# Router logits carried through the attention as eight extra columns, memory scaled on its way out of PSUM

## The chip, the cores and the metric

The kernel runs on one core of a Trainium2 chip. The metric is device time in microseconds, from one launch to its end, and lower is better. TensorE (PE in the profile) multiplies matrices, with its weight loads shown apart as PEld; VectorE (DVE), ScalarE (ACT) and GpSimd (POOL) work element by element; SyncE (SP) issues most transfers. Matrix products land in PSUM and are copied or consumed from there. PSUM buffers are few: the tag `pm` of the pool `ps_m` has one, so each user of it waits until the one before has been read.

## The reference, cut to what matters

Three layers follow each other over 4 x 576 = 2304 tokens of 512 values (8 heads of 64).

```python
scores = q @ k.T / 8, causal                      # per batch and head, 576 x 576
local  = softmax(scores) @ v                      # 576 x 64
mem    = (phi(q) @ M_prev) / (phi(q) @ z_prev + 1e-6)   # phi(x) = elu(x) + 1
x      = sigmoid(beta) * mem + (1 - sigmoid(beta)) * local
logits = (x / (|x| + 1e-6)) @ (emb / (|emb| + 1e-6)).T / tau    # 8 experts
token  -> argmax expert, gate = its softmax weight
out1   = gate * relu(x @ w1[e]) @ w2[e]
g      = h * clip(h + 3, 0, 6) / 6,  h = out1 @ w_in ;  out = g @ w_out
```

The routing needs, for each token, the product of its 512 values with eight expert directions. A row of x is a sum over heads of weighted value rows and memory rows, so these products can be formed before or after the attention's sums.

## The kernel before

**Attention, by pairs.** Sixteen pairs (four batches of four) of heads go through nine blocks each: 128 query rows at a time, five blocks for the first head (the fifth holds the last 64 rows of both heads) and four for the second. A block's scores (`mm` in `scores`, lines 291 to 310) go to PSUM, DVE takes the row maxima (`nmx`, line 314), ACT the exponentials (line 320), PE turns them by transposes (line 330), ACT copies the turned tile (`aT`, line 331), and PE sums values: `sumup`, line 344, with `aT` as weights and 65 columns of `vt` as the moving side (64 values and one column that gives the softmax's sum). The fifth block moves both heads' 130 columns. `finish` divides and adds the memory part into `xb` (lines 350 to 362).

**Memory.** `mem_pair` (line 260) forms phi(q) and multiplies it by `mz` (130 columns: 64 and the normaliser, for two heads), three row blocks in one `pm` tile and two in the next. ACT copies the first out of PSUM, DVE the second (line 274); DVE adds the small constant to the normaliser and inverts it (lines 278 and 279), and POOL multiplies the 128 x 640 tile (line 280).

**Routing.** After each pair `route_pair` (line 365) transposes the pair's 128 columns of `xb`, five blocks of rows (line 373), has them copied by ACT and DVE (line 377), and multiplies each by `enT`, the scaled directions, 8 columns wide (line 380, tile `plg`); DVE adds the result into `lgs`. After a batch's fourth pair `route` takes the norms (five ACT squares, a POOL power), scales the logits, finds the expert, and PE ranks the tokens (`prk`, lines 426 to 429) from the one-hot table `ohb` that DVE wrote at line 421. Then it scales `xb` by the gate and POOL scatters the rows. `totals` counts tokens with one more product, `pc`, line 471.

**What sets the order.** The Python loop at the end of `attention` counts steps, one for each block; in a step it issues scores five blocks ahead, a transpose, the sums of the block before, and one piece of each generator in `jobs` (memory) and of the first in `work` (routing); each `yield` ends a piece. A scheduler then reorders instructions on each engine by its own estimates, so code that is adjacent in the loop needn't be adjacent on an engine. Each engine runs its list in order: an instruction that waits holds all behind it. Transfers are issued by SP in order, eight in flight at most.

**Start.** SP loads pair 0, its values, `mz`, the embeddings and then pair 1. Pair 1 is split into high and low parts on ACT, DVE and POOL (`split_pair`, lines 235 to 258) before its scores.

**Feed-forward.** After the attention the first two slots of the experts run (`NEARLY`), and the last batch's routing and the tables of slots run beside them as `tail`, some pieces after each weight tile (`side`). PE is near full from there to the end.

An fp32 product appears as two PE instructions, so the 400 products of `sumup` are 800 rows in the profile, and `plg` has 160; a transpose is one.

Of the kernel before, what the change touches and what calls it, by code (L numbers as in the profile page):

```python
# [17 lines left out]
P = 128  # L18
# [22 lines left out]
EMB, ZERO, GATES, MEM0 = 1, 32, -3, -2  # L41
AT_LOAD, AT_VT, AT_SPLIT, AT_MEM = -19, -15, -11, -4
# [5 lines left out]
def build(nc, tc, qT, kT, v, Mz, beta, emb, tau, wm, w2, out, dbg=None):  # L48
# [31 lines left out]
def attention(nc, tc, rts, g):  # L80


    qT, kT, v, Mz, beta, emb, tau = (g[n] for n in ("qT", "kT", "v", "Mz", "beta", "emb", "tau"))
# [15 lines left out]
    vt_b = [ac.tile([P, NT, 2, D + 1], F32, name=f"vt{i}", tag=f"vt{i}") for i in range(H // 2)]  # L99
# [17 lines left out]

    def load_values(i):
# [6 lines left out]
    W = 2 * (D + 1)  # L125
# [4 lines left out]
    tau8 = ac.tile([E, 1], F32, name="tau8", tag="tau8")  # L130
    loads = {0: load_pair(0)}
# [48 lines left out]
    def gates():  # L180
# [7 lines left out]
        for i, vt in enumerate(vt_b):  # L188
            w = iomg[:, 2 * i:2 * i + 2]
            nc.vector.tensor_copy(vt[:, :4, :, D], w.unsqueeze(1).to_broadcast([P, 4, 2]))  # L190
            nc.vector.tensor_copy(vt[64:, 4, :, D], w[64:])
        for y in range(2):
            r = slice(64 * y, 64 * y + 64)
            z = mz[r, :, 65 * y + 64].rearrange("p (b h) -> p b h", b=B)
            nc.vector.tensor_tensor(z, z, igb[r, y::2].unsqueeze(1).to_broadcast([64, B, H // 2]), ALU.mult)

    enT = r1.tile([P, 4, E], F32, name="enT", tag="enT")

    def embeddings():
        esq = p2.tile([E, DM], F32, name="esq", tag="ph")  # L200
# [6 lines left out]
        nc.vector.tensor_scalar(emb_s, emb_s, ens, None, ALU.mult)  # L207
        pt = ps_m.tile([P, 512], F32, name="pte", tag="pm")
        for c in range(4):
            nc.tensor.transpose(pt[:, c * E:(c + 1) * E], emb_s[:, c * P:(c + 1) * P], ident[:E, :E])  # L210
        nc.vector.tensor_copy(enT.rearrange("p c e -> p (c e)"), pt[:, :4 * E])
# [48 lines left out]
    def mem_pair(i, qp, mem):  # L260
# [6 lines left out]
        nc.vector.tensor_copy(ph[:, S:], ph[:, 4 * P:S])  # L267
# [118 lines left out]
    def route(b, xb, lgs):  # L386
# [5 lines left out]
        for t in range(NT):  # L392
            nc.scalar.activation(sq, xb[:, t], AF.Square, accum_out=ss[:, t:t + 1])
            if t % 2:
                yield
# [748 lines left out]
```

## Time and profile before

| | us |
|---|---|
| median of 3 runs | 1027.35 (1025.5 to 1032.72) |
| the profiled execution | 1024.81 |
| its span, first to last instruction | 1023.1 |
| PE busy | 965.4 (94%) |
| DVE, ACT, POOL busy | 595.7, 503.2, 337.2 |
| mean granted TensorE clock | 0.974 of full speed |

A busy share of PE counts matmuls from start to modelled end, and they overlap, so the price of one is not its listed duration but the distance from one start to the next; the chain of waits shows that when it merges a run of them. The attention takes the first 297 us. The granted clock has two levels, 2.4 GHz (1.00) and 1.2 GHz (0.50).

### The profile page before, as it was taken

The numbers are of one execution on the slowest core, as the hardware profiler recorded it, in microseconds if no ns is written. First come the engines' busy times: TensorE is split into PE (matmuls) and PEld (weight loads), VectorE is DVE, ScalarE is ACT, GpSimd is POOL, SyncE is SP. The second block draws the span as 40 slices with busy tenths as digits, with TensorE's granted clock in tenths as the row PEclk, the third lists the DMA queues.
The fourth block names the chain that finished last, engine by engine and source line by source line (L and its number), as shares of the span: only waits on it lengthen the run. The fifth ranks groups of instructions, "written<-read, shape, count | busy, mean of one in ns | idle before, by whom it ended". The sixth has DMA issues, their size and how long they took to land.

```text
span 1023.1 us, 18922 instructions
## 1 busy us (share of the span) xinstructions
PE 965.4 (94%) x7054; PEld 890.4 (87%) x7054; DVE 595.7 (58%) x1456; ACT 503.2 (49%) x1036; POOL 337.2 (33%) x268
## 2 busy tenths in 40 slices
PE   8999799899988999899899999799999999999995
PEld 7789689788888999899899988789899999989994
DVE  6676867967857776776776896133333332333321
ACT  6678668767666653452454553233333333333331
POOL 4343634633425474672765235200000000000000
PEclk9799879979999999999999999999999999999998
DMA  9675555622168777877777800200000000000000
GB/s 212 149 168 107 141 123 125 163 65 66 68 231 273 262 238 249 301 248 262 285 258 264 281 28 1 3 22 21 3 19 22 1 21 1 22 1 21 22 1 23
DMA packets 75252, 122.03 MB, mean 119 GB/s; under 512 B 39048, under 2 KB 39048, under 8 KB 75152
## 3 DMA queue, kind: packets, MB, share of 16 engines
q1 hardware_dynamic: 71600, 111.29, 37.4%
q0 software_dynamic: 3552, 9.45, 2.6%
q8 instruction: 57, 0.93, 0.4%
q14 instruction: 43, 0.35, 0.1%
HBM read 107.55 MB, written 13.16 MB: 118 GB/s over the span
## 4 chain that ended last, share of the span: by engine, by line
PE 75%; DVE 9%; DMA 7%; issue 3%; ACT 3%; POOL 2%; SPq 1%; POOLq 0%; DVEq 0%; ACTq 0%
PE ph L796 8%; PE ph L795 8%; PE ph L794 8%; PE po L344 7%; PE po L1043 6%; PE po L1045 6%; PE po L1044 6%; PE ptr L330 4%; DMA perm<-tok,posi 3%; PE py L851 3%; PE py L849 3%; PE py L850 3%; PE ps L302 2%; PE plg L380 2%; PE pm L271 2%
## 5 line engine op out<-in xcount | busy, mean ns | idle before, releaser
L1063 DVE SCALAR_TENSOR_TENSOR t<-t,ph 128x256 f32<-128x256 f32 x144 | 60.4, 420 | 165.5 <-ACT t L1061 164.1
L1061 ACT ACTIVATE t<-ph,half 128x256 f32<-128x256 f32 x144 | 68.2, 473 | 162.1 <-PE ph L796 158.9
L786 POOL TENSOR_TENSOR lw<-rw,hw 128x1024 fp32r<-128x1024 f32 x50 | 119.9, 2403 | 77.5 <-ACT hw L785 67.8
L795 PE MATMUL ph<-xh,lo 128*128 128x256 f32 x480 | 134.3, 280 | 0.0
L796 PE MATMUL ph<-xl,hw 128*128 128x256 f32 x468 | 132.3, 283 | 0.0
L1032 POOL DMA_INDIRECT out<-ob,pmt x18 | 17.5, 972 | 346.5 <-DVE ob L1079 308.1
L794 PE MATMUL ph<-xh,hw 128*128 128x256 f32 x448 | 127.7, 285 | 1.8 <-ACT xh L804 1.8
L344 PE MATMUL po<-vt,aT 128*128 128x65 f32 (+1 forms) x800 | 115.6, 279 | 2.0 <-ACT aT L331 1.9
L344 PEld LDWEIGHTS po<-vt,aT 128*128 128x128 f32 x800 | 109.7, 204 | 3.9 <-ACT aT L331 2.9
L1044 PE MATMUL po<-lo,gh 128*128 128x512 f32 x270 | 107.3, 397 | 0.0
L785 ACT CAST hw<-rw 128x1024 fp32r<-128x1024 f32 x72 | 75.5, 1048 | 56.2 <-PE py L851 36.8
L1066 ACT CAST gh<-t 128x256 fp32r<-128x256 f32 x144 | 58.6, 407 | 85.5 <-DVE t L1063 85.4
L1067 DVE TENSOR_TENSOR gl<-t,gh 128x256 fp32r<-128x256 f32 x144 | 61.6, 428 | 63.0 <-ACT gh L1066 63.0
L320 ACT ACTIVATE a<-ps,nmx 128x256 f32<-128x256 f32 (+4 forms) x160 | 81.5, 527 | 31.8 <-DVE nmx L314 27.7
L795 PEld LDWEIGHTS ph<-xh,lo 128*128 128x128 f32 x480 | 91.0, 190 | 4.8
L795 PE MATMUL ph<-xh,lw 128*128 128x256 f32 x320 | 90.7, 283 | 1.6 <-POOL lw L786 1.6
L314 DVE TENSOR_REDUCE nmx<-ps 128x1 f32<-128x256 f32 (+4 forms) x160 | 74.7, 476 | 29.6 <-PE ps L307 19.2
L796 PEld LDWEIGHTS ph<-xl,hw 128*128 128x128 f32 x468 | 89.1, 190 | 0.0
L794 PEld LDWEIGHTS ph<-xh,hw 128*128 128x128 f32 x448 | 85.4, 191 | 3.4 <-ACT xh L804 2.4
L851 PE MATMUL py<-hl,hw 128*128 128x256 f32 x288 | 82.0, 285 | 5.1 <-DVE hl L838 5.0
L331 ACT COPY aT<-ptr 128x128 f32<-128x128 f32 (+2 forms) x144 | 63.8, 444 | 43.7 <-PE ptr L330 42.2
L849 PE MATMUL py<-hh,hw 128*128 128x256 f32 x288 | 82.1, 285 | 0.0
(307 smaller groups left out, 2611.8 us busy)
## 6 DMA issues: line engine op xcount, KB each, us to landing
rw<-in_wm SPq DMA_DIRECT2D x92, 512.0 KB, 4.7
raw<-in_w SPq DMA_DIRECT2D x32, 512.0 KB, 5.7
k<-in_kT SPq DMA_DIRECT2D x30, 256.0 KB, 5.4
q<-in_qT SPq DMA_DIRECT2D x30, 256.0 KB, 5.0
kp<-in_kT SPq DMA_DIRECT2D x16, 288.0 KB, 3.6
qp<-in_qT SPq DMA_DIRECT2D x16, 288.0 KB, 4.2
vt<-in_v SPq DMA_DIRECT2D x32, 128.0 KB, 4.6
lw<-in_wm SPq DMA_DIRECT2D x8, 512.0 KB, 7.2
```

Source lines behind the costliest of these rows:

```text
L314: done["max"] = nc.vector.tensor_reduce(nmx[:, k:k + 1], ps, AX.X, ALU.max, negate=True)
L320: done["exp"] = nc.scalar.activation(a[:, x0:x1], ps, AF.Exp, bias=nmx[:, k:k + 1])
L344: nc.tensor.matmul(o, aT[:, j, :], w, start=(j == 0), stop=(j == t))
L785: st["copy"] = nc.scalar.copy(hi, raw)
L786: st["split"] = eng.tensor_tensor(lo, raw, hi.bitcast(F32), ALU.subtract)
L794: nc.tensor.matmul(ph, a, xh, start=(c == 0), stop=False)
L795: nc.tensor.matmul(ph, b, xh, start=False, stop=False)
L796: nc.tensor.matmul(ph, a, xl, start=False, stop=(c == 3))
L849: nc.tensor.matmul(o, a, hh, start=(f == 0 and d % 2 == 0), stop=False)
L851: nc.tensor.matmul(o, a, hl, start=False, stop=(f == 7 and d % 2 == 1))
L1044: nc.tensor.matmul(po[t], a, lo[:, 512:], start=False, stop=False)
L1061: nc.scalar.activation(t6, ph, AF.Relu, bias=half[:, :1], scale=1.0 / 6.0)
```

## The change

Values get eight columns more: for each head the product of its value rows with the head's part of the expert directions. `vt` rows become 73 wide (64, 8, 1), memory columns 146, and the tile `xb` holds 72 values for each head, of which the last eight are that head's contribution to the logits. `value_logits` makes them on PE from values loaded a second time, turned (`vw`, one buffer, loaded ten steps ahead), five products for each pair, and ACT copies them into `vt`; `memory_logits` makes the memory's once, 16 products, from a turned copy of `M_prev` (`mt`). `route_pair` is gone; `route` sums the eight head contributions by one DVE reduction and multiplies by the norm's inverse and by `scb`, the directions' scale, made once. Memory is no longer copied out of PSUM: DVE adds, inverts and multiplies straight from it, for three and for two row blocks, and POOL's product is gone. The 64-column copy in `mem_pair` goes from DVE to ACT, and the generator has one `yield` more. `route` and `totals` get another `yield` and a mark (`PAUSE`) before their PE products, and in the feed-forward part `side` stops at the mark. Gated rows go through a tile `xg` of their own.

```diff
-EMB, ZERO, GATES, MEM0 = 1, 32, -3, -2
-AT_LOAD, AT_VT, AT_SPLIT, AT_MEM = -19, -15, -11, -4
+DL = D + E
+D1 = DL + 1
+EMB, ZERO, GATES, DIRS, MEM0 = 6, 32, -3, -4, -2
+PAUSE = 1
+AT_LOAD, AT_VT, AT_SPLIT, AT_MEM, AT_VE, AT_VW = -19, -15, -11, -5, -2, -10
...
+    vw = ac.tile([P, NT * P], F32, name="vw", tag="vw")
+    nc.gpsimd.memset(vw[:, 4 * P:S], 0.0)
+    def load_turned(i):
+        h = slice(i * P, (i + 1) * P)
+        nc.sync.dma_start(out=vw[:, :4 * P], in_=wflat[h, :4 * P])
+        nc.sync.dma_start(out=vw[:, S:], in_=wflat[h, 4 * P:])
...
+    nc.sync.dma_start(out=en, in_=embT)
+    load_turned(0)
     load_values(0)
     nc.sync.dma_start(out=gb, in_=beta.rearrange("(o h) -> o h", o=1).broadcast_to([P, H]))
     for y in range(2):
-        nc.sync.dma_start(out=mz[64 * y:64 * y + 64, :, 65 * y:65 * y + 65], in_=Mz[64 * y:64 * y + 64])
+        nc.sync.dma_start(out=mz[64 * y:64 * y + 64, :, D1 * y:D1 * y + D],
+                          in_=Mz[64 * y:64 * y + 64, :, :D])
+        nc.sync.dma_start(out=mz[64 * y:64 * y + 64, :, D1 * y + DL:D1 * y + D1],
+                          in_=Mz[64 * y:64 * y + 64, :, D:])
+    mt = p2.tile([P, B * H // 2, D], F32, name="mt", tag="k2")
+    nc.sync.dma_start(out=mt, in_=MT)
...
+        psc = ps_m.tile([P, E], F32, name="psc", tag="pm")
+        nc.tensor.matmul(psc, onef, diag, start=True, stop=True)
+        nc.vector.tensor_copy(scb, psc)
+    def directions():
+        for y in range(2):
+            r = slice(64 * y, 64 * y + 64)
+            nc.gpsimd.tensor_copy(en2[r, :, E * y:E * y + E], en[r])
+    def memory_logits():
+        pme = ps_m.tile([D, B * H // 2, 2 * E], F32, name="pme", tag="pm")
+        for i in range(B * H // 2):
+            nc.tensor.matmul(pme[:, i], mt[:, i, :], en2[:, i % (H // 2), :], start=True, stop=True)
+        for y in range(2):
+            nc.vector.tensor_copy(mz[64 * y:64 * y + 64, :, D1 * y + D:D1 * y + DL], pme[:, :, E * y:E * y + E])
+    def value_logits(i):
+        pve = ps_m.tile([P, NT, 2, E], F32, name="pve", tag="pm")
+        for j in range(NT):
+            nc.tensor.matmul(pve[:, j].rearrange("p y e -> p (y e)"), vw[:, j * P:(j + 1) * P],
+                             en2[:, i % (H // 2), :], start=True, stop=True)
+        nc.scalar.copy(vt_b[i % (H // 2)][:, :, :, D:DL], pve)
...
-        nc.vector.tensor_copy(ph[:, S:], ph[:, 4 * P:S])
+        nc.scalar.copy(ph[:, S:], ph[:, 4 * P:S])
+        yield
+        h = 2 * i % H
+        rn = p2.tile([P, NT, 2], F32, name="rn", tag="rn")
         for lo, hi in ((0, 3), (3, 5)):
+            w = hi - lo
             pm = ps_m.tile([P, 512], F32, name="pm", tag="pm")
             for t in range(lo, hi):
-                nc.tensor.matmul(pm[:, (t - lo) * W:(t - lo + 1) * W], ph[:, t * P:(t + 1) * P], mz[:, i, :],
-                                 start=True, stop=True)
-            ev = nc.vector.tensor_copy if lo else nc.scalar.copy
-            ev(mem[:, lo:hi].rearrange("p t y d -> p (t y d)"), pm[:, :(hi - lo) * W])
+                nc.tensor.matmul(pm[:, (t - lo) * W:(t - lo + 1) * W], ph[:, t * P:(t + 1) * P], mz[:, i, :], start=True, stop=True)
+            pv = pm[:, :w * W].rearrange("p (t y d) -> p t y d", y=2, d=D1)
+            r = rn[:, lo:hi]
+            nc.vector.tensor_tensor(r, pv[:, :, :, DL], eps_m[:, h:h + 2].unsqueeze(1).to_broadcast([P, w, 2]), ALU.add)
+            nc.vector.reciprocal(r, r)
+            nc.vector.tensor_tensor(mem[:, lo:hi], pv[:, :, :, :DL], r.unsqueeze(3).to_broadcast([P, w, 2, DL]), ALU.mult)
             yield
-        h = 2 * i % H
-        rn = p2.tile([P, NT, 2], F32, name="rn", tag="rn")
-        nc.vector.tensor_tensor(rn, mem[:, :, :, D], eps_m[:, h:h + 2].unsqueeze(1).to_broadcast([P, NT, 2]), ALU.add)
-        nc.vector.reciprocal(rn, rn)
-        nc.gpsimd.tensor_tensor(mem[:, :, :, :D], mem[:, :, :, :D],
-                                rn.unsqueeze(3).to_broadcast([P, NT, 2, D]), ALU.mult)
...
-            nc.vector.scalar_tensor_tensor(xb[:, t, h * D:(h + 1) * D], o[:, t, :D], rs[:, t:t + 1],
-                                           mem[:, t, y, :D], ALU.mult, ALU.add)
+            nc.vector.scalar_tensor_tensor(xb[:, t, h], o[:, t, :DL], rs[:, t:t + 1],
+                                           mem[:, t, y], ALU.mult, ALU.add)
...
-    def route_pair(b, c, xb, lgs):
...
+        lg = r2.tile([P, NT, E], F32, name="lg", tag="lg")
+        nc.vector.tensor_reduce(lg, xb[:, :, :, D:].rearrange("p t h e -> p t e h"), AX.X, ALU.add)
...
-        nc.vector.tensor_tensor(lg, lgs, bc(ss), ALU.mult)
+        nc.vector.tensor_tensor(lg, lg, bc(ss), ALU.mult)
+        nc.vector.tensor_tensor(lg, lg, be(scb), ALU.mult)
...
         nc.vector.tensor_copy(cumb, cum)
+        yield PAUSE
         yield
         prk = ps_m.tile([P, NT, E], F32, name="prk", tag="pm")
         nc.tensor.matmul(prk, ut, ohb, start=True, stop=False)
...
-            nc.vector.tensor_scalar(xb[:r, t, :], xb[:r, t, :], gate[:r, t:t + 1], None, ALU.mult)
+            xg = r2.tile([P, DM], F32, name="xg", tag="xg", bufs=3)
+            nc.vector.tensor_scalar(xg[:r].rearrange("p (h d) -> p h d", d=D), xb[:r, t, :, :D], gate[:r, t:t + 1],
+                                    None, ALU.mult)
             sent.append(nc.gpsimd.indirect_dma_start(
-                xs[:], bass.IndirectOffsetOnAxis(ap=idp[:r, t:t + 1], axis=0), xb[:r, t, :], None))
+                xs[:], bass.IndirectOffsetOnAxis(ap=idp[:r, t:t + 1], axis=0), xg[:r], None))
...
+        yield PAUSE
+        yield
         pc = ps_m.tile([P, E], F32, name="pc", tag="pm")
...
-                work.append(route_pair(bj, pj, xb_b[bj % 2], lgs))
                 if pj == H // 2 - 1:
-                    work.append(route(bj, xb_b[bj % 2], lgs))
+                    work.append(route(bj, xb_b[bj % 2]))
...
-            embeddings()
+            jobs.append(embeddings())
+        if n == DIRS:
+            directions()
+        if n == MEM0:
+            memory_logits()
+            value_logits(0)
...
-        for at, act in ((AT_LOAD, load), (AT_VT, values), (AT_SPLIT, split), (AT_MEM, mem)):
+        for at, act in ((AT_LOAD, load), (AT_VT, values), (AT_SPLIT, split), (AT_MEM, mem),
+                        (AT_VE, value_logits), (AT_VW, load_turned)):
...
-            for _ in range(4 if k == 0 else 3):
-                next(tail, 0)
+            for _ in range(STEPS):
+                if next(tail, 0) == PAUSE:
+                    break
```

The scheduler's order shows where the new pieces stand. **On PE, around a memory product in the middle of a batch.** Before (`pm` memory, `pxt` the transposes of routing, `plg` the logits, `ps` scores, `ptr` transposed exponentials, `po` value sums):

```order
L271 MATMUL pm<-mz,ph 128x130 [waits DVE_49]
L271 MATMUL pm<-mz,ph 128x130 x2
L373 MATMUL pxt<-ident,xb_238 128x128 [waits Activation_49]
L373 MATMUL pxt<-ident,xb_238 128x128
L305 MATMUL ps<-kp,q_240 128x320 [waits DMAHW6_49]
L305 MATMUL ps<-kp,q_240 128x256 [waits Activation_49]
L380 MATMUL plg<-enT,xT 128x8 [waits Activation_49]
L380 MATMUL plg<-enT,xT 128x8 x2
L309 LDWEIGHTS identb
L309 MATMUL ps<-negm_209,identb 128x64
L330 MATMUL ptr<-ident,a_1916 128x128 x4
```

The change (`pve` the value logits, in the same PSUM buffer as `pm`):

```order
L324 MATMUL pm<-mz,ph 128x146 x3
L354 MATMUL ps<-kp,q_253 128x320 [waits DMAHW1_49,PE_49]
L354 MATMUL ps<-kp,q_253 128x256 [waits PE_49,Activation_49]
L358 LDWEIGHTS identb
L358 MATMUL ps<-negm_221,identb 128x64
L379 MATMUL ptr<-ident,a_2164 128x128 [waits PE_49]
L379 MATMUL ptr<-ident,a_2164 128x128
L259 MATMUL pve<-en_134,vw 128x16 [waits DMAHW2_49,DVE_49,PE_49]
L259 MATMUL pve<-en_134,vw 128x16 x3
L259 MATMUL pve<-en_134,vw 128x16 [waits DMAHW3_49]
L379 MATMUL ptr<-ident,a_2164 128x128 x2
```

Where `plg` waited for ACT to empty `pm`, `pve` waits for DVE, which now does three operations on it. Two rows of value sums later stands the second `pm`, and it waits for ACT to copy `pve`.

**On DVE, ahead of the first batch's one-hot table** (`nmx` maxima, `rs` and `xb` the end of a block, `cand`, `oh`, `ohb` routing). Before:

```order
L411 TENSOR_TENSOR lg<-lg,mx 128x40 [waits DVE_49]
L278 TENSOR_TENSOR rn<-mem_236,eps_m 128x10 [waits DVE_49]
L246 TENSOR_SCALAR q_240<-qp 64x64 [waits DMAHW7_49]
L413 SCALAR_TENSOR_TENSOR cand<-lg,io_m 128x40 [waits DVE_49]
L279 RECIPROCAL rn<-rn 128x10 [waits DVE_49]
L415 TENSOR_REDUCE first<-cand 128x5 [waits DVE_49]
L350 TENSOR_SCALAR rs_243<-po,eps_l 128x4 [waits PE_49]
L416 TENSOR_TENSOR cand<-first,io_m 128x40 [waits DVE_49]
L354 TENSOR_SCALAR rs_243<-po,eps_l 64x1
L418 TENSOR_TENSOR oh<-cand,valid 128x40 [waits DVE_49]
L354 TENSOR_SCALAR rs_243<-po,eps_l 64x1
L421 CAST ohb<-oh 128x40 [waits DVE_49]
```

The change:

```order
L363 TENSOR_REDUCE nmx<-ps 128x1 [waits PE_49,Activation_49]
L439 TENSOR_TENSOR lg<-lg,mx 128x40 [waits DVE_49]
L441 SCALAR_TENSOR_TENSOR cand<-lg,io_m 128x40 [waits DVE_49]
L443 TENSOR_REDUCE first<-cand 128x5 [waits DVE_49]
L363 TENSOR_REDUCE nmx<-ps 128x1 [waits PE_49,Activation_49]
L444 TENSOR_TENSOR cand<-first,io_m 128x40 [waits DVE_49]
L363 TENSOR_REDUCE nmx<-ps 128x1 [waits PE_49]
L446 TENSOR_TENSOR oh<-cand,valid 128x40 [waits DVE_49]
L367 TENSOR_REDUCE nmx<-nmx 128x1 [waits DVE_49]
L449 CAST ohb<-oh 128x40 [waits DVE_49]
```

The memory's and the block end's operations no longer stand between the logits and `ohb`; three maxima do, which the attention needs anyway.

## Rows read from the trace of the kernel before

**Rows 1.** The page: its first line, and bandwidth in 40 slices.

```profile
span 1023.1 us, 18922 instructions
...
GB/s 212 149 168 107 141 123 125 163 65 66 68 231 273 262 238 249 301 248 262 285 258 264 281 28 1 3 22 21 3 19 22 1 21 1 22 1 21 22 1 23
```

**Rows 2.** Attention by window: length, PE, PEld, DVE, ACT, POOL busy, clock, DMA.

```profile
0.00:297.00 297.00, 275.21 (x2106) 244.90 (x2106) 217.85 (x742) 207.46 (x469) 126.31 (x143) 0.94 0.55 134
```

**Rows 3.** PE groups of the whole execution: busy us, mean ns, idle before, releaser.

```profile
L271 PE MATMUL pm<-mz,ph 128*128 128x130 f32 x160 | 27.6, 297 | 0.0
L380 PE MATMUL plg<-enT,xT 128*128 128x8 f32 x160 | 22.8, 258 | 3.7 <-ACT mem L274 2.1 <-ACT xT L377 1.5
L344 PE MATMUL po<-vt,aT 128*128 128x130 f32 x160 | 21.9, 285 | 0.1
...
L426 PE MATMUL prk<-ohb,ut 128*128 128x40 bf16 x4 | 0.8, 199 | 9.3 <-DVE ohb L421 9.3
...
L471 PE MATMUL pc<-cb,ones 128*128 128x8 bf16 x2 | 0.4, 182 | 2.1 <-DVE cb L469 2.1
```

**Rows 4.** Chain of waits, 60 to 100 us: start us, us on the chain, what.

```profile
68.92 2.06 DVE rn L278
...
75.47 0.62 PE plg L380 x6
...
77.21 0.84 PE po L344 x8
...
78.97 1.12 PE po L344 x10
...
82.23 0.72 PE pm L271 x6
82.95 0.97 PE ps L305 x4
...
88.71 0.22 PE pxt L373 x2
...
97.58 0.72 PE pm L271 x6
```

**Rows 5.** Timeline of PE: start, us, what, [idle before, releaser].

```profile
37.09 0.83 PE L380 MATMUL plg<-enT,xT 128*128 128x8 f32 x6 [0.94 <-ACT xT L377]
...
107.45 0.22 PE L426 MATMUL prk<-ohb,ut 128*128 128x40 bf16 x1 [4.23 <-DVE ohb L421]
...
139.03 0.84 PE L380 MATMUL plg<-enT,xT 128*128 128x8 f32 x6 [1.45 <-ACT mem L274]
...
211.29 0.83 PE L380 MATMUL plg<-enT,xT 128*128 128x8 f32 x6 [0.63 <-ACT mem L274]
```

**Rows 6.** Windows again: two at the lower clock, one at the higher.

```profile
37.90:48.20 10.30, 10.30 (x49) 9.35 (x48) 4.11 (x15) 4.54 (x11) 2.14 (x1) 0.50 0.63 130
106.20:113.00 6.80, 5.55 (x29) 4.72 (x30) 5.62 (x26) 3.23 (x7) 0.43 (x1) 0.50 0.84 160
...
60.00:100.00 40.00, 38.43 (x322) 34.71 (x321) 27.14 (x89) 31.50 (x74) 14.94 (x10) 1.00 0.68 138
```

**Rows 7.** DVE and ACT groups, first 300 us, by shape.

```profile
L278 DVE TENSOR_TENSOR rn<-mem,eps_m 128x10 f32<-128x10 f32 x16 | 12.2, 764 | 0.6
...
L279 DVE RECIPROCAL rn<-rn 128x10 f32<-128x10 f32 x16 | 3.2, 202 | 0.1
...
L805 DVE TENSOR_TENSOR xl<-px,xh 128x512 fp32r<-128x512 f32 x2 | 1.3, 686 | 0.0
...
L433 DVE TENSOR_TENSOR pr<-prk,io_r 128x40 f32<-128x40 f32 x3 | 0.5, 172 | 0.0
...
L331 ACT COPY aT<-ptr 128x128 f32<-128x128 f32 x32 | 8.5, 265 | 8.7 <-PE ptr L330 8.4
```

**Rows 8.** Tile q, first 26 us: issues, first use, landing.

```profile
L115 SPq DMA_DIRECT2D q<-in_qT x4: 601/606/612, 8.3 to 17.8; - x4
...
L243 ACT ACTIVATE q<-q x1: 1060/1060/1060, 23.7 to 23.7; 128x1024 f32<-128x1024 f32 x1
...
DMA to landing us min/median/max: 6.2/7.6/7.6
```

More of the change, by code (lines that the diff above doesn't have):

```diff
@@ L98, in attention @@
     vflat = v.rearrange("b h s d -> (b h) s d")
-    vt_b = [ac.tile([P, NT, 2, D + 1], F32, name=f"vt{i}", tag=f"vt{i}") for i in range(H // 2)]
+    wflat = vT.rearrange("b h d s -> (b h d) s")
+    vt_b = [ac.tile([P, NT, 2, D1], F32, name=f"vt{i}", tag=f"vt{i}") for i in range(H // 2)]
     for vt in vt_b:
@@ L206, in embeddings @@
         nc.vector.reciprocal(ens, ens)
[L207 to L211, printed above, removed]
+        onef = ac.tile([E, P], F32, name="onef", tag="onef")
+        nc.vector.memset(onef, 1.0)
+        diag = ac.tile([E, E], F32, name="diag", tag="diag")
+        nc.vector.tensor_scalar(diag, ident[:E, :E], ens, None, ALU.mult)
+        yield
[19 more added lines that the diff above has]
+        nc.scalar.copy(vt_b[i % (H // 2)][:, :, :, D:DL], pve)
     def clear(row, n):
@@ L361, in finish, with route @@
                 r, e = slice(64 * z, 64 * z + 64), (4 + z) * D1
[L362 to L391 removed]
+                nc.vector.scalar_tensor_tensor(xb[:64, 4, h - 1 + z], po[r, e:e + DL],
+                                               rs[r, 4:5], mem[r, 4, z], ALU.mult, ALU.add)
+    def route(b, xb):
+        ss = r2.tile([P, NT], F32, name="ss", tag="ss")
+        sq = r2.tile([P, H, D], F32, name="sq", tag="xg", bufs=3)
+        yield
         for t in range(NT):
[L393 removed]
+            nc.scalar.activation(sq, xb[:, t, :, :D], AF.Square, accum_out=ss[:, t:t + 1])
             if t % 2:
                 yield
+        lg = r2.tile([P, NT, E], F32, name="lg", tag="lg")
+        nc.vector.tensor_reduce(lg, xb[:, :, :, D:].rearrange("p t h e -> p t e h"), AX.X, ALU.add)
         nc.gpsimd.tensor_tensor(ss, ss, half, ALU.pow)
@@ L478, in early_slots @@
     def early_slots():
-        rem = totals()
+        rem = yield from totals()
         ef = r1.tile([P, 4, NEARLY], F32, name="ef", tag="ef")
@@ L542, in slot_tables @@
     def slot_tables():
-        cnt = totals()
+        cnt = yield from totals()
         last = r2.tile([P, E], F32, name="last", tag="last")
@@ L618, in slot_tables @@
         shq = [P, B * NT, NEARLY + NREST]
-        m1 = r1.tile(shq, F32, name="m1", tag="m1")
-        m2 = r1.tile(shq, F32, name="m2", tag="m2")
+        nq = shq[1] * shq[2]
+        m1, m2 = (xb_b[B % 2].rearrange("p t h d -> p (t h d)")[:, k * nq:(k + 1) * nq]
+                  .rearrange("p (q s) -> p q s", s=shq[2]) for k in range(2))
         kf = key.rearrange("p b t -> p (b t)")
@@ L972, in side @@
         if s < 0:
-            for _ in range(4 if k == 0 else 3):
-                next(tail, 0)
+            for _ in range(STEPS):
+                if next(tail, 0) == PAUSE:
+                    break
             if (k, f) == FIRST:
-                assert next(tail, 1)
+                assert next(tail, "end") == "end"
                 open_rest()
```

70 lines of the change are left out of this document (25 added, 45 removed).

## The prediction

> **What bounds the kernel now.** I read the page's first lines, then PE's idle time by group, then the chain of waits in a calm stretch, and last the stretches in which TensorE's clock fell. The reader is to see that the change touches the first 297 us, the attention, and a little of what follows: there PE is busy 275 us, DVE 218 and ACT 207 [rows 2], so PE leads and is short of nothing else by much. The chain at full clock shows the pace: from one memory product to the next, one pair, 97.58 - 82.23 = 15.4 us [rows 4]. Sixteen such pairs are 246 us, and some 12 go to the start, so about 39 of the 297 us are standstill and slow clock. Part of that is PE's idle time, 297 - 275 = 22 us [rows 2]. The rest is the clock: the granted clock is 0.50, that is 1.2 GHz, in four stretches, three of 10.2 us and one of 6.8, of which one of each length stands in [rows 6]. In the long one PE makes 49 instructions in 10.3 us, 4.8 per us, beside 322 in 40 us, 8.1 per us, at 2.4 GHz [rows 6]: it loses 10.3 x (1 - 4.8/8.1) = 4.2 us. The short one loses about 2 beyond its idle time. Together 14.6 us. What stood ahead of each fall: three times PE waited for the router's product `plg` (0.94, 1.45 and 0.63 us), once for `prk` (4.23) [rows 5]. So waits that look small are paid for again.
>
> **The change part by part.**
> *Transposes gone.* Five in each of 16 pairs; two take 0.22 us on the chain [rows 4], so 80 x 0.11 = -8.8 us of PE.
> *Logit products.* 160 passes of `plg` at 0.62/6 = 0.103 us [rows 3, 4] go, and 160 of `pve` come with the same weights' width and as narrow a moving side: 0. The work is renamed, not saved.
> *Columns.* A pass of 65 columns takes 0.84/8 = 0.105 us, one of 130 takes 1.12/10 = 0.112 [rows 4]: below some width the weights set the pace. What a column costs when it does count: the four passes of L305 move 2 x 320 + 2 x 256 columns in 0.97 us, 0.84 ns each [rows 4]. 73 columns are 61 ns, under 105, so 640 passes cost nothing more (bounds 0 and 640 x 8 x 0.84 ns = 4.3). 146 columns are 123 ns, over 112: 160 passes of `sumup` and 160 of `pm` [rows 3] cost 320 x 11 ns = +3.5.
> *Memory's logits.* Once, 32 passes with half as many weight columns; by `plg` 32 x 0.103 = +3.3, by half of it 1.7. The scale `scb` replaces four small transposes. I take +3.
> *The waits for `plg`* were 3.7 us [rows 3]: -3.7.
> *New waits in the one `pm` buffer.* Per pair: `pm`, then DVE adds, inverts, multiplies, then `pve`, then ACT's copy, then `pm` again. DVE's part is 0.17 (L433, a small sum out of PSUM) + 0.20 (L279) + about 0.60 for 432 columns (512 take 0.69, L805) [rows 7], near 1.0 us; ACT's is under 0.27 [rows 7]. In the order PE has 0.97 us of scores and two transposes (0.22) between `pm` and `pve`: nearly enough. Uncovered entirely it would be 16 x 1.2 = 19 us, covered entirely 0; I take 0.25 for each pair, +4, nearer to the covered end since in most pairs more rows stand between.
> *`prk` and `pc`* held PE 9.3 + 2.1 = 11.4 us [rows 3], while DVE worked through the routing chain mixed with the memory's operations. In the new order these no longer stand ahead of `ohb`, but two or three maxima do, and PE still reaches `prk` with little work in hand. Bounds 0 and -11.4; I take half, -5.7. In the feed-forward part the stop at the mark helps the same two products, which is within this term.
> *DVE's blocked sums.* A sum of 128 x 10, both sides in SBUF (L278), takes 0.76 us on average and once 2.06 on the chain, where a sum four times as wide out of PSUM takes 0.17 [rows 4, 7]. It now reads PSUM: -1.9 once for the time it was on the chain; in the others PE had work.
> By the Trainium skill (SBUF — State Buffer, "Who interferes with whom"), a DVE instruction with two SBUF inputs contends with a GpSimd instruction that reads SBUF, and the second to start blocks fully. By that rule, which the two rows bear out, this part gains, but the change's extra product `lg` x `scb` in each batch is exposed to it: the fourth rival.
> *DVE, ACT and POOL otherwise.* ACT loses two copies and gains two smaller ones in each pair, POOL loses its product; none of the three bounds the stage, so 0.
> *Clock.* If the waits for `plg` go, three of the four falls lose what stood ahead of them; the new waits can bring some back. Of 14.6 us I take half, -7; bounds 0 and -14.6, and a loss is a rival.
> *Start.* SP loads about 0.84 MB more before pair 1 (turned values, `mt`, `en`), at 212 GB/s [rows 1] 4 us. Pair 1's queries are issued from 8.3 us, the second half some 1.3 us later, and land 7.6 later, at 17.2; ACT needs them at 23.7 [rows 8]. So 6 us are spare, 4 are used; the 4-byte columns of the normaliser and six more issues of 0.6 us [rows 8] may use the rest. +1, bounds 0 and +5. Later each `vw` load waits on SP until the pair before has been read, with the next pair's values and the loads two pairs ahead behind it; those have some 18 steps, about 30 us at 1.7 a step, so 0.
>
> Sum: -8.8 + 3.5 + 3 - 3.7 + 4 - 5.7 - 1.9 - 7 + 1 = -15.6. The profiled execution took 1024.8, so 1009.2; the median of the runs shown is 2.5 above it, which gives **1012**.
>
> **The rivals.**
> *1. Given back inside the pair.* The new waits cost 0.6 a pair (+10 in place of +4), they stand ahead of the clock's falls as `plg` did (0 in place of -7), and `prk` gives 2 instead of 5.7: -15.6 + 6 + 7 + 3.7 = +1, about 1028. For it: the buffer is one before and after, and DVE was late at 139 us, where a wait of 1.45 stood [rows 5]. Against it: the order leaves work between, and DVE has less to do. Chance 0.25.
> *2. Slower: the handover becomes the pace.* If DVE, behind its maxima, reaches `pm` so late that PE stands 1.2 us in most pairs (+15 over the forecast's +4), then the clock falls more often than now: two falls more in place of -7 are +15. Sum -15.6 + 15 + 15 + 5.7 (nothing gained at `prk`) = +20, about 1047. It decides where PE's work between `pm` and `pve` is under DVE's 1.0 us plus its delay; in the piece of order shown they are about equal, so a steady delay of half a us would do. Chance 0.10.
> *3. More: all waits of this kind go.* `prk` and `pc` give all 11.4 and the clock all 14.6, the new waits 2 instead of 4: -15.6 - 5.7 - 7.6 - 2 = -31, about 996. For it: three of four falls had the same cause, and it is removed. Against: at 107 us the cause was another. Chance 0.16.
> *4. The routing chain gets longer.* One two-input product more stands in it for each batch; if it is held as L278 was, 2.06 us each [rows 4], `prk` waits 4 x 1.9 = 7.6 more than without, and gains nothing: -15.6 + 5.7 + 7.6 = -2, about 1025. Chance 0.07. It is the skill's rule of the page above that would make this happen.
> That the change does not shorten PE's work at all is nearly so: products and columns sum to -2.3. The forecast rests on waits and clock, not on work.
>
> **How the numbers follow.** Forecast 0.42 (1012, its own range 1002 to 1019), rivals 0.25, 0.10, 0.16 and 0.07. About 1% is what a measurement of this kernel can tell from no change. Faster by over 1% means below 1017.1: 0.9 of the forecast, all of rival 3, a little of rival 1: 0.55. Slower, above 1037.6: rival 2 and a tail of rival 1, 0.12. The rest, 0.33. The range that leaves out 2 in 10 cuts half of rival 3 below and rival 2 above: 996 to 1033.
>
> **What would show it.** In the new profile: the passes of 146 columns at 0.12 us on the chain and those of 73 at 0.105; `pve` as dear as `plg`; PE's idle time at `pve` and the second `pm` near 4 us in all, behind DVE and ACT; at `prk` and `pc` under 6; fewer than four stretches at the lower clock; the first pair's scores after the start within 2 us of before. The prediction is wrong if the clock falls as often as before, if the idle time at `pve` and `pm` passes 10 us, or if the attention ends later than 290 us.

## The result, and the profile after

The changed kernel takes 1038.76 us (median of 10 runs, 1034.87 to 1047.16), the kernel before 1028.42 beside it (10 runs, 1021.56 to 1032.93): 1.0115 times before, 95% interval 1.0075 to 1.0155. The forecast was 1012, faster, with a range of 996 to 1033. The profiled execution is the longest of the ten, 1047.16 us; what is read from it is checked below against variants. (A ratio leaves out runs over 1.5% above the fastest of their kernel; that removes three of e11's ten runs, two of e9's ten, two of e13's twelve, one of e8's ten and up to two of the kernel before's, so for e9 and e11 the medians of all runs are given beside it.)

The page of the changed kernel, its first line and the clock granted in 40 slices, to be held against [rows 1]:

```profile
span 1045.4 us, 18802 instructions
...
PEclk8789899789798999999999999989999999999998
```

Windows of the changed kernel (length, PE, PEld, DVE, ACT, POOL busy, clock, DMA share, GB/s), the first as in [rows 2]; the second is the whole attention, whose last sum ends at 316.7 us in place of 294.7; the third a stretch at the start:

```profile
0.00:297.00 297.00, 272.33 (x1925) 241.40 (x1925) 206.96 (x698) 186.59 (x443) 103.37 (x130) 0.87 0.57 135
0.00:318.00 318.00, 292.89 (x2086) 259.32 (x2086) 219.09 (x751) 199.01 (x471) 104.77 (x131) 0.88 0.57 141
19.20:29.50 10.30, 10.27 (x46) 9.98 (x46) 2.44 (x10) 2.56 (x8) 0.00 (x0) 0.50 1.15 202
```

In the same 297 us PE is as busy as before and does less, 1925 recorded matmuls beside 2106; DVE, ACT and POOL are all less busy. What grew is slow clock, 0.87 in place of 0.94.

PE's groups, to be held against [rows 3] (busy us, mean ns, idle before, releaser):

```profile
L393 PE MATMUL po<-vt,aT 128*128 128x73 f32 x640 | 98.5, 289 | 2.1 <-ACT aT L380 2.0
L324 PE MATMUL pm<-mz,ph 128*128 128x146 f32 x160 | 33.3, 340 | 2.2 <-DVE ph L315 2.1
L259 PE MATMUL pve<-en,vw 128*128 128x16 f32 x160 | 23.8, 284 | 1.0 <-DVE pr L462 0.8
L354 PE MATMUL ps<-kp,q 128*128 128x320 f32 x32 | 13.2, 498 | 2.4 <-ACT a L369 2.4
L354 PE MATMUL ps<-kp,q 128*128 128x256 f32 x32 | 11.4, 441 | 3.4 <-ACT a L369 3.3
L251 PE MATMUL pme<-en,mt 128*64 128x16 f32 x32 | 2.0, 210 | 0.0
L455 PE MATMUL prk<-ohb,ut 128*128 128x40 bf16 x4 | 0.8, 198 | 8.7 <-DVE ohb L449 8.7
L504 PE MATMUL pc<-cb,ones 128*128 128x8 bf16 x2 | 0.4, 205 | 1.3 <-DVE mem L329 1.3
```

The 3.7 us of waits for `plg` are gone. `prk` still waits 8.7 us (9.3 before), and 5.8 us of waiting stand at L354, scores that wait for a free PSUM buffer, that is for ACT's exponential. Before, the same line (L305) waited 0.6 us in all.

**Behind L354.** One such wait, in the timeline of DVE, ACT and PE of the changed kernel (start, us, what, [idle before, releaser]):

```profile
204.81 0.48 DVE L482 TENSOR_SCALAR xg<-xb,gate 64x512 f32<-64x512 f32 x1 [3.61 <-DMA xs<-xg,idp]
...
206.45 1.05 ACT L369 ACTIVATE a<-ps,nmx 128x256 f32<-128x256 f32 x2 [2.90 <-DVE nmx L363]
...
206.98 2.29 PE L354 MATMUL ps<-kp,q 128*128 128x320 f32 x4 [2.39 <-ACT a L369]
```

It is read from the top. DVE stands 3.61 us because the gate's product of a tile (L482) now goes to `xg`, of which there are three (the squares of `route` take a turn in the same three), and the scatter DMA still reads the one it wants. Behind it in DVE's order stand maxima, ACT's exponentials wait for these, and PE for the exponentials. From 206.94 the clock is at 1.2 GHz for 10.2 us. Before, the product went back into `xb` and waited for nobody. DVE waits so once more in the attention, and PE's other long wait at L354 (2.60 us at 261.9) has another source:

```profile
127.29 0.49 DVE L482 TENSOR_SCALAR xg<-xb,gate 128x512 f32<-128x512 f32 x1 [3.85 <-DMA xs<-xg,idp]
...
258.02 0.17 DVE L426 TENSOR_SCALAR ss<-ss 128x5 f32<-128x5 f32 x1 [2.23 <-POOL ss L424]
```

Behind the first stands `ph`, for which PE then waits 2.09 us at 128.6. In the second DVE waits for POOL's power in the routing's norm, with the maxima behind it; e5, without the staging, keeps 1.82 us of that wait at 242.0.

**At the start.** PE's timeline of the changed kernel:

```profile
16.27 2.04 PE L251 MATMUL pme<-en,mt 128*64 128x16 f32 x32
...
19.03 2.12 PE L259 MATMUL pve<-en,vw 128*128 128x16 f32 x10
...
23.51 4.53 PE L393 MATMUL po<-vt,aT 128*128 128x73 f32 x20
...
36.14 0.96 PE L351 MATMUL ps<-kx,qx 128*128 128x128 f32 x3 [1.49 <-DVE rs L404]
38.53 0.48 PE L352 MATMUL ps<-kx,ql 128*128 128x128 f32 x1 [1.43 <-POOL ql L306]
```

All sums of the first pair stand behind `pme` and `pve` and run in a lump at the lower clock. The second pair's split on ACT stands behind the copies for these sums, so its scores begin at 36.1 us, where before they began at 25.7.

### The profile page after: what moved, and what is told of

It reads as the page before. It is cut to its first block, busy times and chain, and to the rows that moved or that the text cites. A ratio compares the mean times of both kernels' runs of the same rounds, so it can differ in the third digit from the quotient of the medians.

```text
span 1045.4 us, 18802 instructions
## 1 busy us (share of the span) xinstructions
PE 985.5 (94%) x7004; PEld 907.7 (87%) x7004; DVE 594.9 (57%) x1467; ACT 495.1 (47%) x1036; POOL 315.0 (30%) x256
## 4 chain that ended last, share of the span: by engine, by line
PE 60%; DMA 7%; DVE 6%; issue 3%; ACT 2%; POOL 1%; SPq 1%; ACTq 0%; POOLq 0%; DVEq 0%
PE ph L833 9%; PE ph L832 8%; PE ph L831 8%; PE po L1082 6%; PE po L1084 5%; PE po L1083 5%; DMA perm<-tok,posi 3%; PE py L888 3%; PE py L887 3%; PE py L886 3%; PE po L393 3%; DMA rw<-in_wm 1%; PE ptr L379 1%; DMA raw<-in_w 1%; DMA xs<-xg,idp 1%
## 5 line engine op out<-in xcount | busy, mean ns | idle before, releaser
L393 PE MATMUL po<-vt,aT 128*128 128x73 f32 (+1 forms) x800 | 123.6, 292 | 2.1 <-ACT aT L380 2.0
L393 PEld LDWEIGHTS po<-vt,aT 128*128 128x128 f32 x800 | 115.6, 212 | 4.2 <-ACT aT L380 2.9
L887 PE MATMUL py<-hh,lw 128*128 128x256 f32 x288 | 81.7, 284 | 0.0
```

What stands on the lines that cost most here:

```text
L393: nc.tensor.matmul(o, aT[:, j, :], w, start=(j == 0), stop=(j == t))
L887: nc.tensor.matmul(o, b, hh, start=False, stop=False)
```

## Experiments

Three theories. **S**: the start, as just read. **X**: the staging `xg`. **W**: something spread over all pairs, with the clock. Medians; the ratio is to the runs of before beside them.

**e1: where the time goes.** `memory_logits()` and `value_logits(0)` are not called and their loads go. Since logits are missing, tokens go to other experts and the feed-forward part is another (1528.39 us in all); only its attention is read.

> The changed kernel without what it puts between the first pair's scores and sums: the memory's logits for all pairs (32 passes, the load of the turned memory) and the first pair's value logits (10 passes) are left out, so these logits are taken as zero; everything from the second pair on is unchanged. Theory S (the start: these products and the order behind them, with the clock that fell at 19 us, cost 10 of the 11.8 us): 8 to 12 us below the changed kernel, 1026 to 1031, level with before; the first pass of 146 columns near 21 us, as before, in place of 27. Theory W (the loss is made in the steady part, where waits and slow clock came back behind other engines): only the products themselves go, 2 to 4 us, 1035 to 1037, ratio to before 1.006 to 1.01, and some 50 us or more at the lower clock between 50 and 317 us.

The first sum of values over both heads' columns comes at 21.7 us (27.3 in the changed kernel, 21.2 before), the last sum ends at 308.0 in place of 316.7. So in these two profiles 8.7 us were the start's, as S says: the stretches at the lower clock from 49.9 us on come again, each 8.7 us sooner. But the steady part repeats all its waits: the scores of L354 (L351 there) wait 2.48 us at 198 and 2.59 at 253.

**e5 and e6: the staging, from both sides.** e5 takes its wait out of the changed kernel: each gated row block but the first goes into the columns of `xb` that were read just before, and the squares get a tile of their own. e6 puts the wait into the kernel before; to make room, two late tables (`m1`, `m2`) lie in `xb` there, as in e10, e15 and e16, of which e16 lost nothing.

```diff
-            xg = r2.tile([P, DM], F32, name="xg", tag="xg", bufs=3)
+            xg = xb[:, t - 1]...[:, :DM] if t else r2.tile([P, DM], F32, name="xg", tag="xg", bufs=1)
```

> The changed kernel, but the gate's products are no longer written to the three turning tiles xg (which the squares sq share), where DVE stood 3.6 to 3.9 us for the fourth tile until the scatter had read the first: the first product goes to a tile of its own, each later one into the columns of xb that the product before it has read, and sq has its own tile. Everything else is the changed kernel. Theory X (the staging's wait on DVE, and the falls of the clock behind it, make the loss in the steady part): 12 to 22 us below the changed kernel, 1017 to 1027, and DVE's idle time of 3.6 to 3.9 us before xg is gone. Theory S (the start): the start is untouched, 1036 to 1041. Theory W (wider columns and new waits spread over all pairs): 1033 to 1039.

> The kernel before with the staging alone: the gate's product of each tile goes to one of three turning tiles xg, shared with the squares, in place of back into xb; m1 and m2 lie in xb's room to make place. Theory X: four batches with a wait of near 3.6 us on DVE, of which PE feels 2 or more, and a fall of the clock behind some: 5 to 20 us more than before, 1034 to 1049. Theories S and W: within 3 us of before, 1026 to 1032.

e5: 1032.61 us, 1.0051 (1.0016 to 1.0086), 6 below the changed kernel. e6: 1034.48, 1.0063 (1.0035 to 1.0091). DVE's rows for this line, of the changed kernel, of e5 and of e6, first 318 us:

```profile
L482 DVE TENSOR_SCALAR xg<-xb,gate 128x512 f32<-128x512 f32 x12 | 5.7, 482 | 4.0 <-DMA xs<-xg,idp 3.9
L482 DVE TENSOR_SCALAR xg<-xb,gate 64x512 f32<-64x512 f32 x3 | 1.4, 471 | 3.6 <-DMA xs<-xg,idp 3.6
```

```profile
L482 DVE TENSOR_SCALAR xb<-xb,gate 128x512 f32<-128x512 f32 x10 | 4.8, 482 | 0.1
```

```profile
L453 DVE TENSOR_SCALAR xg<-xb,gate 128x512 f32<-128x512 f32 x12 | 6.8, 568 | 2.1 <-DMA xs<-xg,idp 2.1
```

X holds as to time: the wait is there with three tiles and gone without, and staging costs some 6 us on either kernel. It is about half of the change's loss, less than expected of e5. The path is shown for the changed kernel alone. In e6, DVE's waits in the attention bring no wait of PE; those of the last batch, in the feed-forward part, stand ahead of one:

```profile
332.62 0.48 DVE L453 TENSOR_SCALAR xg<-xb,gate 64x512 f32<-64x512 f32 x1 [1.15 <-DMA xs<-xg,idp]
...
339.05 0.58 PE L853 MATMUL py<-hl,hw 128*128 128x256 f32 x1 [5.25 <-DVE hl L840]
```

Before, PE stood 1.32 us for the same tile `hl`; but e5, without the staging's wait, stands 3.98 there, so how much of the 5.25 is the staging's isn't shown.

**e10 and e15: the start alone, and start and staging together**, put into the kernel before; the products go to tiles that nobody reads.

```diff
+        if n == MEM0:
+            memory_logits()
+            value_logits(0)
```

> The kernel before with the change's start alone: the same loads (turned values, directions, turned memory) at the same place and the same 42 products for the memory and the first pair, whose results go to tiles that nobody reads; m1 and m2 lie in xb's room. Theory S: the second pair's scores start some 8 us later, 1035 to 1041. Theory W: only the products' 3 us, 1030 to 1034.

> The kernel before with the staging of e6 and the start of e10 together; the products' results go to tiles that nobody reads. If the two add up (0.6 and 0.2%): 1.008 times before, near 1037 to 1040, which leaves the rest of the change, the columns, the memory and the pauses, at 0 to +4 us in sum. If a start that is late takes the scatters out of step with the waits: less than 1.006 or more than 1.011.

e10: 1033.80, 1.002 (0.998 to 1.0059). e15: 1040.03, 1.0085 (1.0056 to 1.0114). The second pair's scores in e10:

```profile
37.35 1.08 PE L343 MATMUL ps<-kx,qx 128*128 128x128 f32 x3 [2.48 <-DVE rs L396]
```

The delay of S is there, 11.7 us after the time of before, yet the end is only 0.2% later, which can't be told from none: the later pairs make most of the delay up. The time is what W expected, under S's 1035 to 1041. Start and staging add up (0.63 + 0.2 = 0.83%), in size most of the changed kernel's 1.15%; but the change's other parts gain when they stand alone (below), so a loss that no single part shows is left.

**e2, e7, e9, e12, e13: other starts.** Of the changed kernel, e2 keeps 2 of 32 passes at the start and loads the rest later. e7 (on e5) also loads the second pair first. e9 (on e5) loads from POOL's queue, e13 (on e5) from ACT's; e12 is e9 without the pauses.

```diff
-    nc.sync.dma_start(out=en, in_=embT)
-    load_turned(0)
+    nc.scalar.dma_start(out=en, in_=embT)
+    load_turned(0, nc.scalar)
```

> The changed kernel with all its work, but of the memory's logits only those of the first pair (2 passes) stand ahead of the first pair's sums, loaded by themselves; the other 30 passes come in three parts at later steps, and their load comes after the second pair's. Theory S: 3 to 8 us below the changed kernel, 1031 to 1036, and the first fall of the clock at 19 us is gone or shorter. Theory W: the same products at another place, within 2 us of the changed kernel, 1037 to 1041.

> The changed kernel without the staging's wait, as in e5, and with a start in another order: the second pair's loads go ahead of the gates', the memory's and the directions' loads, and the memory's logits of 15 of 16 pairs come in three parts after the first pair's first sums. Theory S: 5 to 11 us below e5. Theory X alone: within 3 us of e5. Both right: 1008 to 1018.

> e5 with a lighter start: the directions, the first turned values, the normaliser's columns and the turned memory are loaded from POOL's queue, so that the second pair's loads are issued from SP as early as in the kernel before, and the memory's logits of pairs 2 to 15 come in one piece ten steps later. Theory S (what stands ahead of the first pair's sums and delays the second pair's split costs 8 to 10 us): 4 to 10 us below e5's 1032.6, that is 1023 to 1029, and the scores of the second pair start near 30 us in place of 35. Theory W: 1030 to 1035.

> e9 and e11 together. Theories S and P: 1015 to 1023, below the kernel before. S alone: 1023 to 1030. P alone: the same as e11.

> e5 with a start that keeps POOL and SP free: the directions, the first turned values and the first two pairs' slice of the turned memory are loaded from ACT's queue before ACT has other work, the rest of the turned memory after the second pair's loads; 4 of the 32 products for the memory stand at the start, 28 come ten steps later. The first pair's sums then stand among its scores again, as before the change. Theory S: PE is not in a lump at the lower clock between 19 and 30 us, the second pair's third-tile mark comes 5 us or more earlier than e5's 52.5, and the time is 4 to 9 us below e5, 1023 to 1028. If the later pairs make up for whatever the start loses or gains (e10 was 9 us late at that mark and 2 us at the end): within 3 us of e5, 1029 to 1035.

e2: 1049.23, 1.0215 (1.0159 to 1.0271). e7: 1037.68, 1.0102 (1.0051 to 1.0153). e9: 1030.22 beside 1032.10 (0.998 by these medians; 0.9926, 0.988 to 0.9971, as a ratio). e12: 1038.06, 1.0057 (1.0023 to 1.0091). e13: 1034.57, 1.0039 (1.0004 to 1.0073). Four of the five brought waits of their own: e2 stands 2.73 us at 30, with 17.1 us at the lower clock from 46.6; e7 4.96 us at 12.7, since ACT stands 6.0 us for the second pair's queries; e9 and e12 as these rows of e9 show, since POOL issues loads before it makes the mask:

```profile
9.03 0.33 PE L359 MATMUL ps<-negm,identb 128*128 128x128 bf16 x3 [1.95 <-POOL negm L179]
11.25 1.81 PE L352 MATMUL ps<-kp,qs 64*128 64x512 f32 x2 [1.89 <-ACT a L372]
```

Only e13 does what it was meant to; its second pair and e5's:

```profile
27.25 0.65 PE L354 MATMUL ps<-kx,qx 128*128 128x128 f32 x3
```

```profile
32.69 0.65 PE L351 MATMUL ps<-kx,qx 128*128 128x128 f32 x3 [1.49 <-DVE rs L404]
```

It is 5.4 us earlier there, though the mark that was named (the second pair's first sum over both heads' columns) comes at 52.5 as in e5: a wait of 1.68 us at 39.6 and 13.7 us at the lower clock took the gain. At the end it is level with e5. So S is right on where time goes at the start, but mending it gave nothing in e13. In e9 it may have given something: 0.5% against e5 by the medians, 1.2% by the ratios. With ten runs from 1019.02 to 1039.23 that stays open.

**e3, e4, e18, e8, e16: parts alone, in the kernel before.** e3: the pauses. e4: the memory out of PSUM, with the added step. e18: the same without that step. e8: e3 and e4. e16: eight columns of zeros in values, memory and sums.

```diff
-            ev = nc.vector.tensor_copy if lo else nc.scalar.copy
-            ev(mem[:, lo:hi].rearrange("p t y d -> p (t y d)"), pm[:, :(hi - lo) * W])
+            nc.vector.tensor_tensor(r, pv[:, :, :, D], eps_m..., ALU.add)
+            nc.vector.reciprocal(r, r)
+            nc.vector.tensor_tensor(mem[:, lo:hi, :, :D], pv[:, :, :, :D], r..., ALU.mult)
```

> The kernel before with the change's other pauses alone: two steps of the order between the routing's last write and the products prk and pc, and in the feed-forward part a stop at that mark. Theory S: the steady parts of the change are worth something, and this one 2 to 6 us: 1022 to 1026. Theory W: what prk no longer waits for is waited for elsewhere, 1027 to 1030.

> The kernel before with the change's treatment of the memory alone: pm is read and scaled by DVE out of PSUM in both parts, the copy of ph is on ACT, POOL has no product, one step more of the order between ph and pm. Theory S: 0 to 3 us gained, 1025 to 1028. Theory W: pm is held longer, waits and falls of the clock come with it, 1031 to 1036, with some 20 us more at the lower clock than before.

> e4 (the kernel before with the memory scaled out of PSUM, 0.989 of before) without its one step more of the order between ph and pm, so that the operations alone differ from before. If the operations make the gain (no blocked sums, nothing on POOL, DVE's copy gone): 0.986 to 0.993 again. If the order that e4 happened to get makes it: 0.995 to 1.003.

> The kernel before with the memory's scaling out of PSUM and the pauses in routing and totals, that is the change without its eight columns, their products, and the staging. If the two parts add up (0.9892 x 0.9983): 1014 to 1018. All theories expect this; what the changed kernel loses against it is then due to columns, start and staging: 21 to 25 us.

> The kernel before with the eight columns alone: values, memory and sums are 73 and 146 wide, the eight columns hold zeros and nobody reads them; routing, start and scaling are those of before. The forecast's term for the columns, +3.5 us of PE: 1.003 times before (1.000 to 1.006), with a mean granted clock as before (0.967). If the wider sums are what makes the clock fall more often in the changed kernel (0.9585): 1.006 to 1.010, clock 0.963 or less.

e3: 1026.79, 0.9983 (0.9943 to 1.0023). e4: 1017.09, 0.9892 (0.9836 to 0.9948). e18: 1016.95, 0.9898 (0.9866 to 0.993). e8: 1026.81, 0.9974 (0.9936 to 1.0013). e16: 1024.13, 0.9938 (0.9908 to 0.9967). e18, PE's groups, the DVE operation that took the place of L278 in [rows 7], and its attention's window:

```profile
L274 PE MATMUL pm<-mz,ph 128*128 128x130 f32 x160 | 25.9, 291 | 0.3 <-DVE mem L280 0.2
L380 PE MATMUL plg<-enT,xT 128*128 128x8 f32 x160 | 21.6, 253 | 1.4 <-DVE mem L280 0.9 <-ACT xT L377 0.5
L426 PE MATMUL prk<-ohb,ut 128*128 128x40 bf16 x4 | 0.8, 190 | 4.5 <-DVE ohb L421 4.5
```

```profile
L278 DVE TENSOR_TENSOR rn<-pm,eps_m 128x6 f32<-128x6 f32 x16 | 2.6, 161 | 8.2 <-PE pm L274 6.9 <-PE ps L309 1.1
```

```profile
0.00:276.00 276.00, 263.35 (x2092) 233.23 (x2093) 209.59 (x763) 201.46 (x465) 104.24 (x126) 0.97 0.58 141
```

Scaling the memory out of PSUM is by itself the version that beats both kernels, by 1.0% of before, whatever the step: the operations make the gain. The sum takes 161 ns in place of 764, `prk` waits half as long (4.5 for 9.3 us), `plg` 1.4 for 3.7, the clock is 0.97. In its profile the attention ends 18.3 us sooner and the kernel 14.7, since the feed-forward part grows from 728.4 to 732.1 us. With the pauses added (e8) most of the gain is lost, against 1014 to 1018 expected, while the pauses alone (e3) can't be told from no change. The columns alone cost nothing and even gained 0.6%, which is the clock's (table below: 1007.5 without its share, 1006.6 before). So gains of parts don't add up here.

**e11, e14: without the pauses.** e11 is e5, e14 is e13, each with the steps of before.

> e5 without the pauses in routing, totals and the feed-forward part, which go back to the steps of the kernel before. The pauses gave 0.2% where they stood alone, and the memory's scaling lost 0.8% when they were added to it. Theory P (the pauses, once the memory is scaled out of PSUM, move the waits for prk to other products and do harm): 4 to 9 us below e5, 1023 to 1028. Otherwise: 0 to 4 us above it, since prk waits again.

> e13 without the pauses. If the pauses do neither good nor harm once the staging is gone (e11 against e5): within 3 us of e13. If they harm: 4 us or more below e13.

e11: 1031.93 beside 1032.10 of before (0.9998 by these medians; 0.9932, 0.9883 to 0.9982, as a ratio). e14: 1034.28, 1.0031 (0.9997 to 1.0065). Three pairs differ by the pauses, and they disagree: without them e11 is faster than e5 (by 1.2% as ratios, 0.3% by medians), e14 is level with e13, and e12 is slower than e9 (by 1.3 and 0.8%). P isn't shown, and no steady effect of the pauses is.

**e17: empty work ahead of `prk`.**

```diff
+        for _ in range(FILL):
+            nc.tensor.matmul(prk, ones, ones[:, :NT * E]..., start=True, stop=True)
```

> e5 with 48 empty products of 40 columns ahead of each prk, some 2.8 us of PE's time, four times: PE works where it stood 4.1, 3.0 and 1.0 us for ohb. If the standstill ahead of prk is what lowers the clock behind it: the mean granted clock rises from e5's 0.957 to 0.963 or more, and the time is 0 to 5 us below e5's 1032.6 although up to 4 us of empty work are added where there was no wait. If the clock falls for another reason: clock as in e5, 2 to 6 us above it.

1043.18, 1.0141 (1.0094 to 1.0187), clock 0.957. PE's timeline:

```profile
172.21 1.11 PE L457 MATMUL prk<-ones 128*128 128x40 bf16 x38
173.16 0.79 PE L355 MATMUL ps<-kp,q 128*128 128x320 f32 x2
177.83 0.19 PE L458 MATMUL prk<-ohb,ut 128*128 128x40 bf16 x1 [3.88 <-DVE ohb L450]
```

That is 10.6 us above e5, more than either theory said. It does not decide on the clock: the products took half the time meant, PE did them early, and the wait stayed at 3.88, since DVE's chain waits for PE's scores in between.

**The clock, over all runs.** Among the runs of one kernel, those with a lower mean granted clock are longer. Fitted over all runs but e1's, each us of full-speed time lost, (1 - clock) x span, goes with 0.71 us. With that share taken off the mean, what is left scatters by only 1 to 3 us within most kernels (4 to 5 in e9 and e13):

| kernel | runs | mean us | mean clock | without the clock's share |
|---|---|---|---|---|
| before, all comparisons | 116 | 1030.8 | 0.9670 | 1006.6 |
| changed | 10 | 1039.8 | 0.9585 | 1009.1 |
| e5, no staging wait | 10 | 1032.9 | 0.9571 | 1001.3 |
| e6, before + staging | 9 | 1034.5 | 0.9634 | 1007.6 |
| e10, before + start | 10 | 1035.2 | 0.9683 | 1011.8 |
| e15, before + both | 12 | 1039.5 | 0.9682 | 1015.9 |
| e8, before + memory, pauses | 10 | 1027.0 | 0.9730 | 1007.2 |
| e16, before + columns | 12 | 1024.1 | 0.9772 | 1007.5 |
| e18, before + memory | 8 | 1017.0 | 0.9730 | 997.5 |
| e9, e5 + lighter start | 10 | 1028.7 | 0.9687 | 1005.8 |
| e11, e5 - pauses | 10 | 1030.7 | 0.9670 | 1006.5 |

By this the changed kernel's loss is 2.5 us of work and waits and 6.5 us of clock (0.71 x (43.1 - 34.0)). It is a correlation, not an intervention: e17, meant as one, failed. The kernel before goes from 1005.0 to 1007.8 in its five comparisons, so differences of 2 or 3 us in the last column say little. e9 and e11 have the clock of before again, and 4 to 5 us more of work and waits than e5: what came back at one end was lost at the other.

## Why the forecast was wrong

**Its own proofs.** The passes came as forecast: from start to start at full clock, medians of 112 ns for 73 columns (112 for 65 before), 124 for 146, 112 for `pve`; `pme` took 2.04 us of 3. `pve` and `pm` waited 3.2 us, forecast 4, and 2.1 of that was for `ph`, the product's own input, not the buffer: the handover of the one `pm` buffer (rivals 1 and 2) is not the cause. Rival 1 also misread a row: at 139 us PE waited for ACT's copy (`mem` L274), not for DVE. Of the three conditions that were to prove the forecast wrong, that one did not come, the other two did: the clock fell more often (75 us at the lower clock up to 318, 37.5 before), and the attention ended at 316.7, after 290.

**"DVE, ACT and POOL otherwise ... 0."** This step failed. It looked at how busy the engines are and not at what the new tile `xg` waits for; no term of the sum has it. Staging gave +6 us, shown from both sides.

**"`prk` and `pc` ... -5.7."** They gave -1.4 (8.7 + 1.3 for 11.4). The pauses moved the products, but the chain that they wait for is slowed elsewhere. DVE and POOL of the changed kernel, ahead of `prk` at 187.13:

```profile
182.30 2.12 DVE L444 TENSOR_TENSOR cand<-first,io_m 128x40 f32<-128x40 f32 x1
...
184.68 1.08 DVE L446 TENSOR_TENSOR oh<-cand,valid 128x40 f32<-128x40 f32 x1
...
185.84 1.24 DVE L449 CAST ohb<-oh 128x40 bf16<-128x40 f32 x1
...
182.02 2.34 POOL L306 TENSOR_TENSOR ql<-q,qx 128x1024 fp32r<-128x1024 f32 x1 [3.54 <-DVE first L443]
184.44 2.60 POOL L305 TENSOR_TENSOR kx<-k,kx 64x512 fp32r<-64x512 f32 x2
187.13 0.19 PE L455 MATMUL prk<-ohb,ut 128*128 128x40 bf16 x1 [4.07 <-DVE ohb L449]
```

Operations that take 0.2 us elsewhere end with POOL's products: 2.12 + 1.08 + 1.24, some 3.8 us more, nearly all of the 4.07. That is rival 4's mechanism, in other instructions than the one it named (`lg` x `scb` took 0.19, 0.19, 0.70 and 0.20 us), and already there before the change: `cand` took 1.24 us at 105.5 there, beside POOL's memory product. By the Trainium skill (SBUF — State Buffer, "Who interferes with whom") a DVE operation with two SBUF inputs contends with a GpSimd instruction that reads SBUF, and a cast can where it runs in a 2-port mode; whichever issues first has the shared ports for the whole instruction. The trace agrees for the first two: POOL started first, and `cand` and `oh` end within 0.1 us of its products. The cast ends so too (187.08, POOL 187.04), but no run shows the mode it ran in.

**"Start ... +1."** As a mechanism this step failed. It counted SP's queue and DMA slack, not that 42 passes stand between the first pair's scores and its sums, with the second pair's split behind. The second pair was 10 us late. What it costs at the end is less, 5.2 us without the clock's share (e10), but 0.2% in all, within the noise, and e13 did not win it back. So the size at the end isn't shown.

**"Clock ... -7."** This step failed, and it is the largest: a size by assumption, and of the wrong sign, +6.5. The waits for `plg` went, but falls now come with waits for `prk`, `ph` and ACT, two of them behind `xg` (at 128.4 and 206.9 us). Of the parts alone only the staging lowered the clock a little (0.963 in e6); the others left it near 0.967 or raised it (e3, e4, e8, e10, e16, e18). Why it falls to 0.957 in e5, when the parts are together, stays open. The value products with the new routing were never run alone.

**The rest** of the sum was forecast at -9.6 (-15.6 without clock and start). Measured without the clock's share: +2.5 for the change, less 7.8 for the staging (changed against e5) and 5.2 for the start, -10.5. As a sum it came out, but not term by term. `prk` and `pc` gave 1.4 of 5.7. The memory's scaling alone, in the kernel before, gives 9.1 (997.5 for 1006.6 in e18), for which the sum had 1.9 under the blocked sums and part of `prk`. No run measured the time of the transposes or of the waits for `plg` alone. The split also hangs on the side: taken from the kernel before (e6), staging costs 1.0 without the clock's share in place of 7.8, and the rest comes to -3.7. By the first reckoning the gap of 25 us (by the means) is 13 of clock, 8 of staging and 4 of start. Only the staging's cost is shown by experiment; the start's and the clock's shares are the fit's word.

## What to carry to other kernels

When a result is moved to a tile of its own, ask first how many there are and what reads them last: a DMA that empties a tile in 4 us makes the fourth write of three wait, on an engine that many others wait for. Of work moved to the start, price the place in each engine's order, not only its loads. And run the parts of a change alone: here one part was worth 1% by itself and the whole lost 1%.

## What was not expected of the hardware

The same program runs at mean granted clocks of 0.955 to 0.980 from run to run, and its time follows, 1021 to 1045 us for the kernel before; one profile is therefore no measure of some 10 us. In e12 the granted clock is shown as 1.00 from 10 to 40 us, yet the six passes of `pm` at 24.1 us took 1.76 us, where six at 76.6 us of the changed kernel took 0.96. The first entry of its clock record stands at 41.8 us, and e9, whose start is the same, shows 0.50 from 11.5 to 42.3: a 1.00 ahead of the first entry is not a measurement. At 19.2 us of the changed kernel the clock fell with no wait of over 0.13 us in the 5 us ahead, after the 32 narrow passes of `pme`.
